# A delta-rule attention and an FFN on one core: raw weights decoded through PSUM, norm temporaries in PSUM, a new written order

## The chip, the core and the metric

The kernel runs on one core of one Trainium2 chip. Five engines work side by side, each through its own instruction queue in order: TensorE (PE, matmuls, with its weight loads shown apart as PEld), VectorE (DVE), ScalarE (ACT), GpSimd (POOL) and SyncE (SP, which here only issues DMAs). Matmuls write to PSUM, which has eight banks of 512 float32 values in each of 128 partitions; all other data lies in SBUF. The metric is device time in microseconds, lower is better. The kernel before takes 664.81 us (median of 3 runs, 664.76 to 665.1).

## The reference

An attention with a state that is updated token by token, and behind it a feed-forward layer on the attention's output:

```python
def _attn_ref(q, k, v, beta):                      # 4 x 8 heads, 768 tokens, 48 features
    k_n = k / (np.linalg.norm(k, axis=-1, keepdims=True) + 1e-06)
    state = np.zeros((B, H, D, D)); y = np.zeros_like(q)
    for t in range(S):
        kt, vt, bt = (k_n[:, :, t], v[:, :, t], beta[:, :, t, None])
        y[:, :, t] = np.einsum('bhd,bhde->bhe', q[:, :, t], state)
        v_old = np.einsum('bhde,bhd->bhe', state, kt)
        state = state + bt[:, :, :, None] * np.einsum('bhd,bhe->bhde', kt, vt - v_old)
    return y

def _moe_ref(x, w_in, w_out):                      # 3072 tokens, 384 -> 2048 -> 384
    h = x @ w_in
    sp = np.maximum(h, 0.0) + np.log1p(np.exp(-np.abs(h)))     # softplus
    g = h * erf(sp)
    return (g @ w_out).astype(np.float32)
```

All of it is float32, and the order of the tokens matters: the state of a head at token t depends on all earlier tokens.

## The kernel before, in words

**Attention.** The 768 tokens are cut into 12 chunks of 64 (index c). For a chunk the kernel forms the Gram matrices of the keys (`gram_mm`, "pg") and of queries with keys ("pq"), scales them by beta and the inverse norms (`gram_a`, `gram_d`), solves a triangular system for each head (POOL's `solve_row`, 31 rows for each pair of chunks; for the first two chunks instead DVE's `first_row`, 15 steps), puts the blocks of the inverse together (`merge_e`, `merge_z`, `merge_m`) and then walks the chain of states: for each chunk and batch (index j, 48 in all) `chain_u`, `chain_s` and `chain_y` on PE, each followed by a step on DVE or ACT (`chain_u2`, `chain_s2`, `chain_y2`).

**Norms.** `norm_sq` (ACT) squares the keys of a chunk, `norm_sum` (DVE) sums the squares, and `norms` (DVE, 18 small operations on 128x32 values for two chunks) takes a bit-trick start value and three root iterations, and from them `nm` (the norm), `ga` and `gn` (beta over the squared norm, plus and minus). The group of two chunks is called sg, 0 to 5.

**Weights.** w_in and w_out come in as float32 pairs read as int64, in 12 blocks each of 128x512 pairs (512 KB). A block goes through four steps: `w_load` (DMA into a raw buffer), `w_mask` (ACT, a Prelu that turns the high words into float values, line 539), `w_low` (DVE, shift of the low words, line 543), `w_bits` (DVE, joins both, line 547). After three blocks `w_sum` (ACT) takes the absolute maximum. Then come a scale (`w_max`, `w_all`, `w_scale`), and 16 parts of each weight are split into two float16 halves: `w_hi`, and for w_in `w_dif` (two float32 matmuls and one float16 on PE into PSUM) and `w_lo` (a copy out).

**FFN.** 12 groups of 256 tokens (index g). `x_tr` transposes the attention's output, `x_all`/`x_scale` scale it, `x_hi` and `x_lo` split it into float16 halves; `ffn1` makes 16 slices of h (nine matmuls each, line 678), two slices in one PSUM tile called ph; ACT takes softplus (`e_sp`, line 704) and erf (`e_erf`, line 709), DVE or ACT copies h (`h_out`, lines 691 and 689), DVE multiplies (`e_mul`) and splits (`e_split`, `e_rest`); `ffn2` multiplies by w_out into the banks pr (lines 739 to 741) and `ffn_out` and `ffn_store` finish.

**PSUM.** Pool psa has three banks (tag pa), ps1 has two (tag ph), and three banks pr0 to pr2 are held throughout. Tag ph serves `warm` (one tile that all the filler matmuls of the start write, held until the last of them), the tiles wd of `w_dif`, and the tiles ph of `ffn1`. An engine that touches a bank waits for another engine that still uses that bank.

**Tables of ACT.** Softplus lies in one table set and erf in another. `table(i)` adds a load where its own record says that another set is loaded; it is called in `e_sp`, `e_erf` and `w_sum`, not in `w_mask`.

**Order.** Every step is recorded as an event, and the table ORDER, a permutation of all 2531 events, sets the order in which they are issued; each engine, SP's DMA queue included, takes its own in that order. Filler matmuls (`fill`, 150 of them, line 143) stand among PE's events of the first 80 us.

Of the kernel before, what the change touches and what calls it, by code (L numbers as in the profile page):

```python
# [7 lines left out]
F32 = mybir.dt.float32  # L8
F16 = mybir.dt.float16
BF16 = mybir.dt.bfloat16  # L10
I32 = mybir.dt.int32
# [4 lines left out]
P = 128  # L16
# [23 lines left out]
WO = 0.6  # L40
WD = 0.4
RI = "HLHLHLHLHLLL"
RO = "HLHLHLHLHLLL"
LMI = [5, 3] * 8
LMO = [0] * 16
WG = 3
LID = 0.12
LOD = 0.25
HQ = (0, 4)
SPA = (2, 6)  # L50
EB = 4
HB, LB = 5, 7
# [20 lines left out]
def delta_ffn_kernel(ctx, tc, kT, qT, ktok, vtok, btok, w_in, w_out, cst, out):  # L73
# [99 lines left out]
    def load_q(c):  # L173
        for hb in range(2):
            sp.dma_start(qp[c % 2][hb][rd(hb)], qT[c, hb])

    def norm_sq(c):
        s = st[c]
        if c < 2:
            s["sq"] = early(4160 + 1024 * c, 1024)[:, :BP * D].rearrange("p (a d) -> p a d", a=BP)  # L180
        else:
            s["sq"] = at.tile([P, BP, C], F32, tag="A", name=f"sq{c}")[:, :, :D]
        se.activation(s["sq"], s["k"], AF.Square, bias=0.0, scale=1.0)

    nt = {}

    def norm_sum(c):
        sg, i = divmod(c, 2)
        if sg not in nt:
            nt[sg] = sm.tile([P, 2, BP], F32, tag="n2", name=f"n2_{sg}")  # L190
        ve.tensor_reduce(nt[sg][:, i, :], st[c]["sq"], axis=AX.X, op=ALU.add)

    def norms(sg, w):

        w = slice(0, 2)
        names = ("ri", "t1", "nm", "ga", "gn")
        if sg not in nb:
            nb[sg] = [sm.tile([P, 2, BP], F32, tag=k, name=f"{k}{sg}") for k in names]
        n2, be = nt[sg][:, w], be_t[sg][:, w]
        ri, t1, nm, ga, gn = (x[:, w] for x in nb[sg])  # L200
        ii = ri.bitcast(I32)
        ops = [lambda: ve.tensor_scalar(n2, n2, 1e-30, None, op0=ALU.max),

               lambda: ve.tensor_scalar(ii, n2.bitcast(I32), 1, None, op0=ALU.logical_shift_right),
               lambda: ve.tensor_scalar(ii, ii, -1.0, float(0x5F3759DF), op0=ALU.mult, op1=ALU.add)]
        for _ in range(3):
            ops += [lambda: ve.tensor_tensor(t1, ri, ri, op=ALU.mult),
                    lambda: ve.scalar_tensor_tensor(t1, t1, -0.5, n2, op0=ALU.mult, op1=ALU.mult),
                    lambda: ve.scalar_tensor_tensor(ri, t1, 1.5, ri, op0=ALU.add, op1=ALU.mult)]
        ops += [lambda: ve.tensor_tensor(nm, n2, ri, op=ALU.mult),  # L210
                lambda: ve.tensor_scalar(nm, nm, 1e-6, None, op0=ALU.add),
                lambda: ve.reciprocal(ri, nm),
                lambda: ve.tensor_tensor(t1, be, ri, op=ALU.mult),
                lambda: ve.scalar_tensor_tensor(gn, t1, -1.0, ri, op0=ALU.mult, op1=ALU.mult),
                lambda: ve.tensor_scalar(ga, gn, -1.0, None, op0=ALU.mult)]
        for i in range(2):
            st[2 * sg + i].update((k, x[:, i, :]) for k, x in zip(names, nb[sg]))
        return ops
# [292 lines left out]
    def stage(nm, i, n=RW):  # L511

        return wb[nm].rearrange("p a b -> p (a b)")[:, DM + i * n:DM + i * n + n]
# [21 lines left out]
    def w_mask(nm, i):  # L535


        hf = wt[nm]["raw", i][:, :, 1].bitcast(F32)
        se.activation(stage(nm, i), hf, AF.Prelu, bias=0.0, scale=2.0 ** -112, alpha=2.0 ** 32)
# [5 lines left out]
    def w_bits(nm, i):  # L545
        ai = stage(nm, i).bitcast(I32)
        ve.scalar_tensor_tensor(ai, ai, 3, wt[nm]["raw", i][:, :, 0], op0=ALU.logical_shift_left, op1=ALU.bitwise_or)
# [450 lines left out]
```

## Time and profile before

| | before |
|---|---|
| median of 3 runs | 664.81 us (664.76 to 665.1) |
| the profiled execution | 663.63 us, its span 661.9 us |
| granted TensorE clock, mean | 0.986 |
| PE busy | 630.6 us (95%), 9866 matmuls |
| DVE busy | 468.8 us (71%), 1032 instructions |
| ACT busy | 468.6 us (71%), 694 instructions |
| POOL busy | 357.7 us (54%), 524 instructions |
| moved by DMA | 56.20 MB |

Line numbers (L678) are those of the kernel before. A row of the group view reads: line, engine, operation, output<-input, shapes, count, then the group's busy time, the mean duration of one in ns, and the idle time of the engine just before them with what ended it. A row of a window reads: the stretch, its length, then the busy time and count of PE, PEld, DVE, ACT and POOL, the granted clock, the share of the DMA engines and GB/s. A row of the timeline or of the chain that ended last begins with the start and the duration, both in us.

### The profile page before, as it was taken

The page shows a single profiled execution, that of the slowest core. Times are in us where ns is not written, and L with a number is a line of the kernel's source. Part 1 is how long each engine was busy: PE and PEld are TensorE (multiplying, and loading weights), DVE is VectorE, ACT ScalarE, POOL GpSimd, SP SyncE. Part 2 cuts the span into 40 slices and gives each one's busy share as a digit, 9 for nine tenths or more (in the row PEclk, how much of TensorE's full clock was granted, in tenths as well). Part 3 has the DMA queues.
Part 4 walks back from the last instruction along what each step waited for, and adds up shares of the span by engine and source line. Part 5 has one row for each costly group of instructions (what it writes and reads, how often), then busy time and mean ns, then how long its engine had stood idle before and what let it go on. Part 6 is the DMA issues. An engine that isn't in the chain of part 4 may idle for free.

```text
span 661.9 us, 22889 instructions
## 1 busy us (share of the span) xinstructions
PE 630.6 (95%) x9866; PEld 481.5 (73%) x9866; DVE 468.8 (71%) x1032; ACT 468.6 (71%) x694; POOL 357.7 (54%) x524
## 2 busy tenths in 40 slices
PE   6788999999999999999899999999999999999996
PEld 4556668777768787777687677887776787777763
DVE  4977869878877886668766778875649765657541
ACT  2187898999768897656684677667566788768860
POOL 5081289779997259782489942239972321211322
PEclk8878999999999999999999999999999999999999
DMA  9875761673121740504622241531204210000102
GB/s 246 283 214 164 195 182 34 127 140 77 39 90 29 164 106 3 126 16 112 146 46 56 76 87 26 127 78 31 52 18 104 46 39 13 14 1 1 37 1 48
DMA packets 76421, 56.20 MB, mean 85 GB/s; under 512 B 57184, under 2 KB 66528, under 8 KB 76320
## 3 DMA queue, kind: packets, MB, share of 16 engines
q1 hardware_dynamic: 76320, 54.74, 33.9%
q8 instruction: 77, 1.26, 0.8%
q14 instruction: 24, 0.20, 0.1%
HBM read 42.14 MB, written 12.58 MB: 83 GB/s over the span
## 4 chain that ended last, share of the span: by engine, by line
PE 53%; DVE 16%; ACT 13%; POOL 7%; issue 5%; DMA 4%; SPq 1%; POOLq 0%; DVEq 0%; ACTq 0%
PE ph L678 17%; PE pr L739 7%; PE pr L741 6%; PE pr L740 6%; DVE H L713 3%; POOL xb L364 3%; ACT L128 3%; POOL tmp L363 2%; PE warm L143 2%; ACT L L709 2%; PE pc L488 2%; DVE H L691 2%; PE pm L426 1%; DVE z L467 1%; ACT L L704 1%
## 5 line engine op out<-in xcount | busy, mean ns | idle before, releaser
L678 PE MATMUL ph<-xh,w_in 128*128 128x256 f16 x1152 | 207.6, 273 | 2.7 <-ACT L L704 2.3
L678 PEld LDWEIGHTS <-w_in 128*128 128x128 f16 x1728 | 164.9, 98 | 30.2 <-issue 3.8
L128 ACT ACT_TABLE_LOAD x131 | 168.1, 1283 | 2.2
L728 POOL TENSOR_TENSOR L<-H,L 128x512 f16<-128x512 f32 x72 | 85.3, 1195 | 147.6 <-DVE L L724 96.7
L678 PE MATMUL ph<-xl,w_in 128*128 128x256 f16 x576 | 157.0, 273 | 0.0
L741 PE MATMUL pr<-w_out,L 128*128 128x384 f16 x384 | 125.2, 326 | 0.7 <-POOL L L728 0.7
L739 PE MATMUL pr<-w_out,L 128*128 128x384 f16 x384 | 125.4, 327 | 0.0
L740 PE MATMUL pr<-w_out,L 128*128 128x384 f16 x384 | 125.2, 326 | 0.0
L448 POOL TENSOR_TENSOR z<-v,nm 64x192 f32<-64x192 f32 x96 | 56.4, 587 | 104.6 <-DMA v<-vtok 59.8
L704 ACT ACTIVATE L<-ph,xct 128x512 f32<-128x512 f32 x96 | 65.7, 687 | 53.5 <-DVE H L691 48.5
L364 POOL TENSOR_TENSOR xb<-xb,tmp 128x31 f32<-128x31 f32 (+15 forms) x155 | 95.0, 613 | 12.2
L363 POOL TENSOR_TENSOR tmp<-gb,xb 128x31 f32<-128x31 f32 (+15 forms) x155 | 85.1, 549 | 27.0 <-DMA gb<-d 16.7
L713 DVE TENSOR_TENSOR H<-H,L 128x512 f32<-128x512 f32 x96 | 75.6, 795 | 27.9 <-ACT L L709 23.6
L691 DVE TENSOR_SCALAR H<-ph 128x512 f32<-128x512 f32 x72 | 49.2, 685 | 36.0 <-PE ph L678 27.5
L709 ACT ACTIVATE L<-L 128x512 f32<-128x512 f32 x96 | 58.6, 627 | 0.8
L741 PEld LDWEIGHTS <-L 128*128 128x128 f16 x384 | 37.6, 98 | 26.1 <-POOL L L728 1.4
L739 PEld LDWEIGHTS <-L 128*128 128x128 f16 x384 | 37.5, 98 | 21.8
L740 PEld LDWEIGHTS <-L 128*128 128x128 f16 x384 | 37.6, 98 | 20.8
L467 DVE TENSOR_TENSOR z<-pc,ga 64x192 f32<-64x192 f32 x80 | 28.4, 355 | 27.5 <-PE pc L461 26.0
L661 ACT ACTIVATE xh<-pt,xsx 64x128 f16<-64x128 f32 (+1 forms) x72 | 26.0, 395 | 24.6 <-PE pt L645 12.7
L143 PE MATMUL warm<-zero 128*128 128x384 f16 x158 | 35.0, 373 | 3.3 <-issue 2.2
L724 DVE CAST L<-H 128x512 f16<-128x512 f32 x72 | 35.7, 500 | 1.4
(157 smaller groups left out, 968.5 us busy)
## 6 DMA issues: line engine op xcount, KB each, us to landing
raw_in<-w_in SPq DMA_DIRECT2D x12, 512.0 KB, 8.0
raw_out<-w_out SPq DMA_DIRECT2D x12, 512.0 KB, 5.0
d<-A SPq DMA_DIRECT2D x20, 256.0 KB, 3.2
kpg<-kT SPq DMA_DIRECT2D x24, 192.0 KB, 4.5
k<-ktok SPq DMA_DIRECT2D x12, 384.0 KB, 4.6
v<-vtok SPq DMA_DIRECT2D x48, 96.0 KB, 2.7
qp<-qT SPq DMA_DIRECT2D x24, 192.0 KB, 3.5
out<-ob SPq DMA_DIRECT2D x48, 96.0 KB, 2.2
```

Of the source, the lines that this page charges most:

```text
L128: se.add_instruction(mybir.InstLoadActFuncSet(name=nc.get_next_instruction_name(), act_func_set_id=i, ins=[], outs=[]))
L363: ge.tensor_tensor(tv, G[:, s, s + 1:].unsqueeze(1).broadcast_to([P, ncol, nr]), Xv[:, :, s:s + 1].broadcast_to([P, ncol, nr]), op=ALU.mult)
L364: ge.tensor_tensor(Xv[:, :, s + 1:], Xv[:, :, s + 1:], tv, op=ALU.add)
L678: te.matmul(ph, w[:, i, kt * P:kt * P + P], G[x][:, :, ksl], start=(m == 0), stop=(m == 8))
L691: ve.tensor_scalar(dst, src, HSC, None, op0=ALU.mult)
L704: se.activation(unit("L", g, u), G["ph", u], AF.Softplus, bias=0.0, scale=G["ct"])
L709: se.activation(Lu, Lu, AF.Erf, bias=0.0, scale=1.0)
L713: ve.tensor_tensor(Hu, Hu, unit("L", g, u), op=ALU.mult)
L728: (ge if (g * NFF // EU + u) % GLM else ve).tensor_tensor(G["gl", u], unit("H", g, u), G["gh", u], op=ALU.subtract)
L739: te.matmul(G["po"][a], gh[:, o, asl], wout_h[:, i, :], start=(i == 0), stop=False)
L740: te.matmul(G["po"][a], gh[:, o, asl], wout_l[:, i, :], start=False, stop=False)
L741: te.matmul(G["po"][a], gl[:, o, asl], wout_h[:, i, :], start=False, stop=(i == NFF - 1))
```

## The change

Three things change. `w_mask` writes its result no longer into the weight's own SBUF space but into a PSUM tile of tag ph (both weights, PM), and `w_bits` takes it from there. The squared norms (n2) and the temporary t1 lie in unused columns of a bank pr (`ntmp`); since no operation then has two PSUM inputs, the root iteration multiplies in another order, with the same count of operations, and `ga` is formed directly. And the table ORDER is another one. All 2531 events are the same.

```diff
-ORDER = (1,56,2,4,88,42,3,23,13,36,5,7,27,6,44,9,10,273,52,130,14,57,37,24,25,43,17, ...
+ORDER = (1,63,7,42,5,14,6,3,8,27,4,77,9,19,65,37,48,64,49,43,2,57,58,44,529,66,10, ...
...
+PM = ('in', 'out')
...
+    def ntmp(sg, k):
+        return pr[sg % PB][:, 384 + 32 * k:416 + 32 * k].rearrange("p (i a) -> p i a", i=2)
+
     def norm_sum(c):
...
-            nt[sg] = sm.tile([P, 2, BP], F32, tag="n2", name=f"n2_{sg}")
+            nt[sg] = ntmp(sg, 0)
...
-            nb[sg] = [sm.tile([P, 2, BP], F32, tag=k, name=f"{k}{sg}") for k in names]
+            nb[sg] = [sm.tile([P, 2, BP], F32, tag=k, name=f"{k}{sg}") if k != "t1" else ntmp(sg, 1) for k in names]
...
-            ops += [lambda: ve.tensor_tensor(t1, ri, ri, op=ALU.mult),
-                    lambda: ve.scalar_tensor_tensor(t1, t1, -0.5, n2, op0=ALU.mult, op1=ALU.mult),
+            ops += [lambda: ve.tensor_tensor(t1, n2, ri, op=ALU.mult),
+                    lambda: ve.scalar_tensor_tensor(t1, t1, -0.5, ri, op0=ALU.mult, op1=ALU.mult),
                     lambda: ve.scalar_tensor_tensor(ri, t1, 1.5, ri, op0=ALU.add, op1=ALU.mult)]
-        ops += [lambda: ve.tensor_tensor(nm, n2, ri, op=ALU.mult),
-                lambda: ve.tensor_scalar(nm, nm, 1e-6, None, op0=ALU.add),
+        ops += [lambda: ve.tensor_tensor(t1, n2, ri, op=ALU.mult),
+                lambda: ve.tensor_scalar(nm, t1, 1e-6, None, op0=ALU.add),
...
-                lambda: ve.scalar_tensor_tensor(gn, t1, -1.0, ri, op0=ALU.mult, op1=ALU.mult),
-                lambda: ve.tensor_scalar(ga, gn, -1.0, None, op0=ALU.mult)]
+                lambda: ve.tensor_tensor(ga, t1, ri, op=ALU.mult),
+                lambda: ve.scalar_tensor_tensor(gn, t1, -1.0, ri, op0=ALU.mult, op1=ALU.mult)]
...
-        se.activation(stage(nm, i), hf, AF.Prelu, bias=0.0, scale=2.0 ** -112, alpha=2.0 ** 32)
+        if nm in PM:
+            dst = wt[nm]["p", i] = ps1.tile([P, RW], F32, tag="ph", name=f"wm_{nm}{i}")
+        else:
+            dst = wt[nm]["p", i] = stage(nm, i)
+        se.activation(dst, hf, AF.Prelu, bias=0.0, scale=2.0 ** -112, alpha=2.0 ** 32)
...
-        ve.scalar_tensor_tensor(ai, ai, 3, wt[nm]["raw", i][:, :, 0], op0=ALU.logical_shift_left, op1=ALU.bitwise_or)
+        ve.scalar_tensor_tensor(ai, wt[nm]["p", i].bitcast(I32), 3, wt[nm]["raw", i][:, :, 0], op0=ALU.logical_shift_left, op1=ALU.bitwise_or)
```

The lines of the changed kernel are up to eight further down: `w_mask` is 547, `w_bits` 555, `ffn1` 686, softplus 712, erf 717.

**ACT in the decoding of w_in.** The first rows are the kernel before, the next the changed one, at the place where ACT decodes the middle blocks of w_in (raw_in) between the small copies that build the first inverse (xm).

```order
L539 ACTIVATE w_in_100<-raw_in11_272 128x512
L539 ACTIVATE w_in_100<-raw_in7_385 128x512
L344 COPY w_out_101<-pw1_508 128x256
L539 ACTIVATE w_in_100<-raw_in8_328 128x512
L333 COPY xm0_0_90<-w_out_101 32x16x32
```

```order
L547 ACTIVATE wm_in8_650<-raw_in8_173 128x512
L547 ACTIVATE wm_in11_657<-raw_in11_328 128x512
L547 ACTIVATE wm_in9_674<-raw_in9_275 128x512
L547 ACTIVATE wm_in6_683<-raw_in6_372 128x512
L337 COPY xm0_1_91<-w_out_101 32x16x32
```

Each output is now a tile wm of tag ph. While `warm` holds one of the two banks, all tiles wm lie in the other one (in the built program 16 in a row, the 12 of w_in and the first 4 of w_out), so a `w_mask` follows the `w_bits` of the block before it.

**DVE at the same place, changed kernel.** The rows that free the bank, each with w_low (line 551) of other blocks between:

```order
L555 SCALAR_TENSOR_TENSOR w_in_100<-wm_in0_440,raw_in0_268 128x512
L551 TENSOR_SCALAR raw_in2_422<-raw_in2_422 128x512
L551 TENSOR_SCALAR raw_out10_259<-raw_out10_259 128x512
L555 SCALAR_TENSOR_TENSOR w_in_100<-wm_in2_572,raw_in2_422 128x512
L551 TENSOR_SCALAR raw_in4_270<-raw_in4_270 128x512
L555 SCALAR_TENSOR_TENSOR w_in_100<-wm_in8_650,raw_in8_173 128x512
L551 TENSOR_SCALAR raw_in11_328<-raw_in11_328 128x512
L555 SCALAR_TENSOR_TENSOR w_in_100<-wm_in11_657,raw_in11_328 128x512
```

What moved: mask and join of one block now alternate across the two engines, block by block, where ACT could run ahead.

**ACT at the first softplus.** Before, from the last sum ahead of the first softplus (L0 from ph0) to the first table load behind it:

```order
L554 ACTIVATE raw_out2_675,mx_out_111<-w_out_101 128x1536
L611 CAST w_in_100<-wd_in11_1680 128x384
L128 ACT_TABLE_LOAD
L704 ACTIVATE L0_0_1741<-ph0_1_1687,xct0_1576 128x512
L704 ACTIVATE L0_0_1741<-ph0_0_1729,xct0_1576 128x512
L689 ACTIVATE H0_0_1724<-ph0_0_1729 128x512
L183 ACTIVATE sq5_1785<-k5_1389 128x16x48
L704 ACTIVATE L0_1_1813<-ph0_2_1758,xct0_1576 128x512
L611 CAST w_in_100<-wd_in12_1787 128x384
```

And in the changed kernel, from the same load on:

```order
L129 ACT_TABLE_LOAD
L712 ACTIVATE L0_0_1772<-ph0_1_1729,xct0_1612 128x512
L547 ACT_TABLE_LOAD
L547 ACTIVATE wm_out9_1787<-raw_out9_1563 128x512
L277 COPY qp0_0_86<-pq2_0_1691 64x512
L277 COPY qp0_1_87<-pq2_0_1691 64x512
L497 COPY y5_1822<-pr2_83 128x192
L712 ACT_TABLE_LOAD
L712 ACTIVATE L0_0_1772<-ph0_0_1760,xct0_1612 128x512
L697 ACTIVATE H0_0_1770<-ph0_0_1760 128x512
L547 ACT_TABLE_LOAD
L547 ACTIVATE wm_out7_1841<-raw_out7_1559 128x512
```

The masks of blocks 9 and 7 of w_out now stand between softpluses; behind the last row come one squaring, a fourth load at line 712 and the softplus of ph0_2. The four loads at lines 547 and 712 are not `table`'s (that is line 129): they are put in when the program is built, since Prelu is not in softplus's set. The built program has 136 table loads; it had 132.

2 lines of the change are left out of this document (1 added, 1 removed).

## The prediction

> **What bounds the kernel now.** I read the busy times first, then windows by stage, then the groups of ACT and DVE with what they waited for, and last the chain at the start.
>
> ```profile
> PE 630.6 (95%) x9866; PEld 481.5 (73%) x9866; DVE 468.8 (71%) x1032; ACT 468.6 (71%) x694; POOL 357.7 (54%) x524
> 0.00:33.00 33.00, 23.65 (x461) 16.10 (x465) 22.20 (x67) 6.21 (x9) 9.61 (x18) 0.90 0.91 265
> 33.00:94.20 61.20, 55.91 (x1342) 37.86 (x1330) 45.88 (x107) 49.61 (x91) 29.82 (x46) 0.92 0.72 198
> 97.00:129.00 32.00, 31.88 (x470) 26.02 (x469) 28.75 (x74) 29.73 (x50) 26.34 (x43) 1.00 0.32 68
> 100.00:650.00 550.00, 538.94 (x7970) 420.05 (x7968) 394.97 (x846) 406.48 (x582) 312.10 (x453) 1.00 0.28 62
> ```
>
> From 100 to 650 us PE is idle for 550 - 538.94 = 11.1 us only, and its work there is the same in both kernels. So the time is set by when PE gets to the FFN, and by what makes it wait afterwards. From 33 to 94 us PE looks busy too, but part of that is filler:
>
> ```profile
> L143 PE MATMUL warm<-zero 128*128 128x384 f16 x158 | 35.0, 373 | 3.3 <-issue 2.2 <-DVE zero L134 1.1
> 99.22 0.27 PE L678 MATMUL ph<-xh,w_in 128*128 128x256 f16 x1
> 94.24 1.10 ACT L661 ACTIVATE xh<-pt,xsx 128x256 f16<-128x256 f32 x3 [0.36 <-DVE xsx L528]
> 128.70 0.33 PE L739 MATMUL pr<-w_out,L 128*128 128x384 f16 x1
> ```
>
> The first real FFN matmul starts at 99.22 us, five microseconds after `x_hi` starts on ACT at 94.24. In front of it ACT worked 49.61 of 61.2 us, so it idled 11.6. What it waited for:
>
> ```profile
> ACT T L405 <- PE pe L400: 4.4, 1, 4.4
> ACT w_out L344 <- PE pw L340: 2.8, 1, 2.8
> ACT w_in L611 <- PE wd_in L604: 1.2, 1, 1.2
> ACT w_in L590 <- ACT xm L417: 0.8, 1, 0.8
> ```
>
> Two waits of 4.4 and 2.8 us are for PE, whose chain there is fillers and instruction issue:
>
> ```profile
> 34.06 1.73 PE warm L143 x10
> 36.14 2.44 issue
> 49.41 2.15 issue
> 51.56 3.66 PE warm L143 x13
> ```
>
> From 97 to 129 us, where the FFN begins, PE is full (31.88 of 32) and ACT has 2.3 us to spare (29.73 of 32). This is the stretch in which a late ACT makes a late PE.
>
> **The change part by part.** All sums are made against the profiled execution, 663.63 us (span 661.9 and 1.7 around it); the median of the runs is 664.81, so 1.2 is added at the end.
>
> *Norms in PSUM.* The 18 operations stay 18. Early, alone, one takes 0.19 us; later it is longer:
>
> ```profile
> L207 DVE TENSOR_TENSOR t<-ri 128x32 f32<-128x32 f32 x18 | 5.6, 310 | 0.5
> L207 DVE TENSOR_TENSOR t<-ri 128x32 f32<-128x32 f32 x3 | 0.6, 191 | 0.1
> L631 DVE TENSOR_REDUCE xm<-sp 128x1 f32<-128x128 f32 x12 | 3.4, 284 | 4.3 <-PE sp L523 4.3
> L499 DVE TENSOR_REDUCE mg<-y 128x1 f32<-128x192 f32 x48 | 14.7, 343 | 0.9 <-ACT y L493 0.7
> ```
>
> If all 18 of line 207 ran at 0.19, DVE would save 18 x 0.12 = 2.1 us over the run, and something on its neighbours. A PSUM input has a price too: no row shows such a small operation on PSUM, and the nearest is the reduction at line 631, 284 ns for 128 values of PSUM against 343 for 192 of SBUF, so between nothing and some 0.06 us each. For sg 0, which lies on the chain, that is 0 to 18 x 0.06 = 1.1 us lost. For sg 1 to 5 it is DVE time, and DVE idles 155 us between 100 and 650. I take nothing, cover: DVE's idle time; if that cover is gone, a few us at most.
>
> *`w_bits` from PSUM.* On DVE:
>
> ```profile
> L547 DVE SCALAR_TENSOR_TENSOR w_in<-w_in,raw_in 128x512 int32<-128x512 int32 x12 | 10.3, 868 | 2.3 <-ACT w_in L539 1.9
> L547 DVE SCALAR_TENSOR_TENSOR w_out<-w_out,raw_out 128x512 int32<-128x512 int32 x12 | 9.1, 770 | 0.5
> L547 DVE SCALAR_TENSOR_TENSOR w_in<-w_in,raw_in x12: 680/692/1569, 24.7 to 62.1; 128x512 int32<-128x512 int32 x12
> ```
>
> Median 692 ns, mean 868 and 770: a few are stretched. At the median throughout DVE saves 12 x 0.18 + 12 x 0.08 = 3.1 us. DVE has 15.3 us of idle time from 33 to 94 us (61.2 - 45.88), so I take none of it as time.
>
> The Trainium skill ("SBUF — State Buffer", Who interferes with whom) says that a VectorE instruction with two SBUF inputs contends with GpSimd's reads, and one with a single SBUF input does not. The stretched `w_bits` and root operations fit that; by it the whole 3.1 us would be saved, which changes no term here since DVE is not what x waits for.
>
> *Start, up to 33 us.* SP now issues both key chunks, beta and both kf ahead of any 512 KB weight block. Before, ACT's first mask held the squares back:
>
> ```profile
> 0.74 0.87 SPq L232 DMA_DIRECT2D kpg<-kT  x2
> 4.11 0.42 PE L247 MATMUL pg<-kpg 48*32 48x64 f32 x2
> 2.12 5.77 DMA raw_in<-w_in
> 7.92 0.66 ACT w_in L539
> 8.58 0.74 ACT w_out L183
> 15.67 2.66 DVE w_out L264 x8
> 18.35 2.12 DVE w_out L316
> 30.82 1.86 DVE w_out L327
> ```
>
> The first kf came 3.4 us after its issue at 0.74; keys issued as the fourth load, at about 2.6, can then be there at 6.0 at the earliest, where the squares started at 8.58: at most 2.6 us earlier, at least nothing, and I take 1.9. DVE's order then differs in front of the two transposes that PE waits for (lines 327 and 329; the one at 30.82 took 1.86 us): two of eight `gram_d` moved behind, two `w_bits` (0.7 each, a row above) moved behind the transposes, and the transpose that `first_w` needs is now the second instead of the first, some 1.9 us that take back the gain. So `first_w` starts at about 32.7 us as before (30.82 + 1.86), while two `w_bits` are still owed. I count zero, bounds -1.5 and +1.
>
> *ACT from 33 us to `x_hi`.* By the two orders ACT has nearly the same work left there:
>
> ```profile
> L611 ACT CAST w_in<-wd_in 128x384 f16<-128x384 f32 x16 | 7.5, 476 | 1.3 <-PE wd_in L604 1.2
> L333 ACT COPY xm<-w_out 32x512 f32<-32x512 f32 x8 | 4.9, 612 | 0.1
> ```
>
> It is one more `norm_sq` (0.74 as in the row at 8.58), one more `w_lo` (line 611, 0.48) and one `first_copy` less (line 333, 0.61), about 50.2 instead of 49.6 us. What changes is idle time. It gains a wait: with one bank for the masks, a mask that stands next to a mask on ACT waits for the `w_bits` between them, about 0.7 us. In the order that is blocks 8 to 11, 11 to 9 and 9 to 6 of w_in, and 3 to 5, 5 to 2 and 8 to 0 of w_out: six, 4.2 us. Behind such a mask stand the copies that build xm, and PE waits for those. It loses a wait: only 68 fillers instead of 96 stand in front of `merge_e(0)` on PE, 28 x 0.17 to 0.33 = 5 to 9 us of PE, more than the 4.4 us that ACT waited for exactly that. The second mask can start when the first `w_bits` is done behind the transposes, at 32.7 + 0.7 = 33.4. I keep 2.0 us of small waits for `w_dif` and its like as now (1.2 + 0.8) and 1.5 for PE's issue stalls. So `x_hi` starts at 33.4 + 50.2 + 4.2 + 2.0 + 1.5 = 91.3 instead of 94.24: **-2.9 us**. Bounds: with the six handoffs alone 87.8 (-6.4); with all of the present 11.6 us of idle time and the handoffs on top 99.4 (+5.2).
>
> *The start of the FFN.* The groups:
>
> ```profile
> L128 ACT ACT_TABLE_LOAD x131 | 168.1, 1283 | 2.2
> L704 ACT ACTIVATE L<-ph,xct 128x512 f32<-128x512 f32 x96 | 65.7, 687 | 53.5 <-DVE H L691 48.5 <-PE ph L678 4.2
> L539 ACT ACTIVATE w_out<-raw_out 128x512 f32<-128x512 f32 x12 | 7.6, 672 | 0.0
> 108.42 1.28 ACT L128 ACT_TABLE_LOAD   x1
> 109.72 0.63 ACT L709 ACTIVATE L<-L 128x512 f32<-128x512 f32 x1
> ```
>
> Four table loads more, 4 x 1.283 = 5.1 us, and one mask more than before behind `x_hi` (block 7, line 539), less the one `w_lo` that is already done (0.48): 5.3 us more on ACT in a stretch where it had 2.3 to spare and PE nothing. Queued behind the masks on ACT are the softplus of ph0_0 and ph0_2 and the `w_lo` of parts 12 and 13; PE's `w_dif` and `ffn1` wait for those. The two masks also hold a bank ph each, from the mask to the end of its `w_bits`, 0.67 + 0.69 = 1.4 us, in which `ffn1` has one bank. Bounds: 5.3 - 2.3 = 3.0 if ACT's spare time takes its share; 5.3 + 2 x 1.4 = 8.1 if the bank waits come on top. I take the loads, **+5.1**, near the middle, since loads and held banks overlap in part.
>
> The Trainium skill ("ScalarE: Activation LUTs", What ACT_TABLE_LOAD costs) gives 1283 ns for a load and some 1380 ns of drain with it, 2.66 us a switch. The trace has the 1283, but the erf at 109.72 starts 0.02 us after its load ended. By the page the four would cost 10.6 us and the sum come out 5.5 higher; the measurement decides.
>
> *The rest of the order.* Outside that stretch the table loads are as many as before. PE's 11.1 us of idle time from 100 to 650 are many small waits:
>
> ```profile
> PE ph L678 <- ACT L L704: 2.3, 4, 0.8
> PE pt L644 <- DVE A L258: 1.5, 2, 1.1
> ```
>
> In another order these are other waits. `norm_sum` of sg 4 and 5 also waits for the last `ffn2` of the group whose bank it uses, and the `h_out` behind it on DVE with it. I take **-0.5** (`gram_a` of chunk 3 comes earlier, so POOL's solve does), bounds -4 and +4.
>
> Sum: -2.9 + 5.1 - 0.5 = +1.7: the profiled execution 665.3, the median 664.81 + 1.7 = **666.5 us**.
>
> **The rivals.**
>
> *Faster: ACT's gain at the start outweighs the loads.* If only the six handoffs remain (-6.4) and ACT's spare time takes its share of the loads (+3.0): -3.4, **661.4 us**. For it speaks that 7.2 of ACT's 11.6 idle us are waits for PE, which now has fewer fillers in its way; against it that 97 to 129 us is already full on PE.
>
> *No change: PE takes the delay back.* If the waits of 100 to 650 us shrink because PE arrives later than the engines that feed it, 2 of the 11.1 us are enough: +1.7 - 2 = about 0, **664.8 us**. Against it: these waits are at most 1.1 us each, and most are for steps that themselves follow PE.
>
> *Clearly slower: the one bank decides the start.* If PE's issue stalls (2.44 and 2.15 us) fall again in front of `merge_e(0)` and `first_x`, ACT keeps some 4.5 of its waits for PE on top of the handoffs: `x_hi` comes at 94.9 to 95.8, about +1.5, and with the loads +6.6: **671 us**. It decides from the point where a mask waits longer than the 0.7 us of one `w_bits`.
>
> **How the numbers follow.** About 0.2% (1.3 us) is what a measurement here can tell from no change. Forecast 0.31, faster 0.31, no change 0.25, clearly slower 0.13. The forecast alone spans 665 to 669; the range over the cases is 661 to 671, since rivals on both sides hold most of the chance. Both slower cases make 0.44; no change 0.25; faster 0.31.
>
> **What would show it.** In the changed profile: 136 table loads; the first `ffn1` near 96 instead of 99.2 us; in the group of `w_mask` idle time that DVE's `w_bits` ended, about 4 us; PE idle for 4 us or more in the 35 us behind the first `ffn1`, with waits for softplus, line 712, or for line 555; the first `ffn2` at 127 to 130 us, with less PE work done in front of it. The forecast is wrong if the first `ffn1` comes before 93 or after 99 us, if PE stays full behind it in spite of the loads, or if PE's idle time from there to 650 us differs from 11 us by more than four beside that stretch.

## The result, and the profile after

The changed kernel takes 672.13 us (median of 11 runs, 666.76 to 674.36); the kernel before, beside it on the same chips, 664.05 us (11 runs). The ratio is 1.0115, 95% interval 1.0092 to 1.0139: slower by 1.15%, some 7.6 us. Forecast were 666.5 us and a range up to 671; the sign was right, the size too small by nearly six microseconds. The profiled execution takes 671.29 us with a span of 669.5, against 663.63 and 661.9 before.

PE by stage, first before and then after, each cut at the first `ffn1`, 34 us behind it and near the end. The columns are the stretch, its length, PE's busy time and count, the granted clock, the share of the DMA engines and GB/s:

```profile
0.00:99.22 99.22, 84.59 (x1854) 0.91 0.76 214
99.22:134.00 34.78, 34.66 (x497) 1.00 0.42 86
134.00:650.00 516.00, 505.06 (x7482) 1.00 0.27 61
650.00:661.90 11.90, 6.30 (x39) 0.91 0.24 54
```

```profile
0.00:103.46 103.46, 87.40 (x1871) 0.90 0.73 206
103.46:138.00 34.54, 29.65 (x421) 1.00 0.33 78
138.00:657.00 519.00, 509.12 (x7534) 1.00 0.27 61
657.00:669.50 12.50, 7.40 (x46) 0.96 0.14 31
```

From the first `ffn1` to the end PE does the same work: 34.66 + 505.06 + 6.30 = 546.0 us before, 29.65 + 509.12 + 7.40 = 546.2 after. So the 7.6 us split into three: the first `ffn1` starts 4.2 us later (103.46 instead of 99.22); in the 34.5 us behind it PE idles 4.9 us instead of 0.1; and from there to the end it idles 15.0 us instead of 16.5.

The starts of `x_hi` and of the first `ffn1` (timeline of the changed kernel), and what ACT waited for from 33 us to `x_hi` (waits: in total, times, longest):

```profile
99.56 2.22 ACT L669 ACTIVATE xh<-pt,xsx 128x256 f16<-128x256 f32 x6 [0.17 <-DVE xsx L532]
103.46 0.27 PE L686 MATMUL ph<-xh,w_in 128*128 128x256 f16 x1
```

```profile
ACT wm_in L547 <- DVE w_in L555: 4.6, 6, 1.6
ACT T L409 <- PE pe L404: 2.9, 1, 2.9
ACT wm_out L547 <- DVE w_out L555: 2.5, 3, 1.0
ACT xm L421 <- PE pz L417: 1.4, 1, 1.4
```

`x_hi` comes at 99.56 us instead of 94.24, where 91.3 was forecast. The handoffs of the masks on their one bank are there, nine instead of six, 7.1 us instead of 4.2. Behind the first `ffn1` PE waits for what was named:

```profile
PE ph L686 <- DVE w_out L555: 2.7, 2, 1.3
PE wd_in L611 <- ACT L L712: 0.9, 1, 0.9
PE spout L527 <- DVE m_out L566: 0.8, 1, 0.8
PE wd_in L611 <- ACT w_in L619: 0.6, 1, 0.6
```

On DVE the joins and the root iteration are faster than before (groups: count, busy time, mean ns, idle time in front):

```profile
L555 DVE SCALAR_TENSOR_TENSOR w_in<-wm_in,raw_in 128x512 int32<-128x512 int32 x12 | 8.3, 688 | 3.8 <-ACT wm_in L547 3.4
L211 DVE TENSOR_TENSOR pr<-pr,ri 128x32 f32<-128x32 f32 x18 | 3.5, 196 | 2.0 <-PE pr L478 1.5
L213 DVE SCALAR_TENSOR_TENSOR ri<-pr,ri 128x32 f32<-128x32 f32 x18 | 3.4, 191 | 0.6
```

A `w_bits` takes 688 ns on average where it took 868, the iteration's operations 0.19 to 0.20 us, where the same groups of before had means of 231 to 349 ns. That gain did not reach the end here; the last experiments show where it can.

### The profile page after: what moved, and what is told of

Its sections match the earlier page's. It is cut to its first block, busy times and chain, and to the rows that moved or that the text cites. A ratio compares the mean times of both kernels' runs of the same rounds, so it can differ in the third digit from the quotient of the medians.

```text
span 669.5 us, 22923 instructions
## 1 busy us (share of the span) xinstructions
PE 633.6 (95%) x9866; PEld 485.2 (72%) x9866; DVE 467.1 (70%) x1032; ACT 474.9 (71%) x698; POOL 356.8 (53%) x524
## 3 DMA queue, kind: packets, MB, share of 16 engines
q8 instruction: 77, 1.26, 0.8%
## 5 line engine op out<-in xcount | busy, mean ns | idle before, releaser
L736 POOL TENSOR_TENSOR L<-H,L 128x512 f16<-128x512 f32 x72 | 87.0, 1220 | 129.2 <-DVE L L732 118.7
L452 POOL TENSOR_TENSOR z<-v,nm 64x192 f32<-64x192 f32 x96 | 54.1, 564 | 113.5 <-DMA v<-vtok 59.3
L367 POOL TENSOR_TENSOR tmp<-gb,xb 128x31 f32<-128x31 f32 (+15 forms) x155 | 88.0, 568 | 42.0 <-DMA gb<-d 32.6
L368 POOL TENSOR_TENSOR xb<-xb,tmp 128x31 f32<-128x31 f32 (+15 forms) x155 | 92.9, 599 | 12.1
L732 DVE CAST L<-H 128x512 f16<-128x512 f32 x72 | 41.1, 572 | 1.8
L471 DVE TENSOR_TENSOR z<-pc,ga 64x192 f32<-64x192 f32 x80 | 28.4, 355 | 18.2 <-PE pc L465 16.5
```

Of the source, the lines that this page charges most:

```text
L367: ge.tensor_tensor(tv, G[:, s, s + 1:].unsqueeze(1).broadcast_to([P, ncol, nr]), Xv[:, :, s:s + 1].broadcast_to([P, ncol, nr]), op=ALU.mult)
L368: ge.tensor_tensor(Xv[:, :, s + 1:], Xv[:, :, s + 1:], tv, op=ALU.add)
L452: ge.tensor_tensor(zz[j % 6][h1, :, hb, :], vt[j][h1], st[c]["nm"][h1, cs].unsqueeze(2).broadcast_to([C, NP, D]), op=ALU.mult)
L736: (ge if (g * NFF // EU + u) % GLM else ve).tensor_tensor(G["gl", u], unit("H", g, u), G["gh", u], op=ALU.subtract)
```

## The experiments

All ratios are to the kernel before on the same chip. "SBUF" and "PSUM" say where masks and norms lie.

| run | edit | median, before beside it | ratio (95%) |
|---|---|---|---|
| changed | | 672.13, 664.05 | 1.0115 (1.0092 to 1.0139) |
| e1 | new order, old code | 670.49, 662.38 | 1.0126 (1.0083 to 1.0169) |
| e2 | changed, masks in SBUF | 671.24, 662.38 | 1.0138 (1.0094 to 1.0183) |
| e3 | changed, norms in SBUF | 669.75, 662.38 | 1.0106 (1.0065 to 1.0148) |
| e4 | changed, two masks ahead of `ffn1` | 668.80, 662.38 | 1.0099 (1.0060 to 1.0137) |
| e5 | old code, old order up to `x_hi` | 668.06, 661.84 | 1.0091 (1.0058 to 1.0125) |
| e6 | old code, new order up to `x_hi` | 665.57, 661.84 | 1.0040 (1.0015 to 1.0065) |
| e7 | changed, 18 fillers out | 666.48, 661.84 | 1.0055 (1.0032 to 1.0077) |
| e8 | old order, norms in PSUM | 662.34, 661.84 | 1.0002 (0.9980 to 1.0025) |
| e9 | changed, load_q(11) early | 669.11, 662.87 | 1.0105 (1.0072 to 1.0138) |
| e10 | changed, two masks under erf's table | 665.79, 662.87 | 1.0050 (1.0021 to 1.0078) |
| e11 | before, 18 fillers out | 663.92, 662.87 | 1.0026 (1.0007 to 1.0045) |
| e12 | e7, e9 and e10 together ("mended") | 662.22, 662.87 | 0.9996 (0.9978 to 1.0014) |
| e13 | mended, w_out's masks in SBUF | 661.88, 661.96 | 1.0004 (0.9980 to 1.0029) |
| e14 | mended order, old code | 666.92, 661.96 | 1.0077 (1.0053 to 1.0100) |
| e15 | e5 with the mask of block 9 late, load_q early | 667.42, 661.96 | 1.0073 (1.0047 to 1.0099) |
| e16 | e13 with norms in SBUF | 666.91, 663.09 | 1.0059 (1.0033 to 1.0085) |
| e17 | e13, w_max(out) ahead of three norm operations | 663.11, 663.09 | 1.0002 (0.9980 to 1.0024) |
| e18 | e17 with the 18 fillers | 665.67, 663.09 | 1.0045 (1.0016 to 1.0075) |

### Which of the three changes costs: e1, e2, e3, e8

e1 takes the kernel before and exchanges only the table:

```diff
-ORDER = (1,56,2,4,88,42,3,23,13,36,5,7,27,6,44,9,10,273,52,130,14,57,37,24,25,43,17, ...
+ORDER = (1,63,7,42,5,14,6,3,8,27,4,77,9,19,65,37,48,64,49,43,2,57,58,44,529,66,10, ...
```

> The kernel before with the new order alone: masks and norms in SBUF as before. The changed kernel started its first ffn1 at 103.46 us (before 99.22) and lost 4.9 us of PE in the 34.5 us behind it. Theory M (the masks' one bank makes ACT wait, 7.1 us for w_bits): without the PSUM masks x_hi comes at 92 to 95, first ffn1 at 97 to 100; the table loads stay, so PE idles 2 to 4 us at the FFN's start; 664 to 667 us. Rival N (norms in PSUM: DVE waits 2.7 and 1.5 us for PE matmuls in the same bank): the same for this kernel, since the norms are in SBUF too. Rival O (the order itself, PE's queue of w_dif and fillers): first ffn1 stays at 102 to 104, 669 to 672 us.

e2 keeps the changed kernel and puts the masks back:

```diff
-PM = ('in', 'out')
+PM = ()
```

> The changed kernel with both kinds of masks written to SBUF again; norms stay in PSUM, the new order stays. Theory M: no wait of ACT for w_bits, x_hi at 92 to 95, first ffn1 97 to 100, the 2.7 us of ffn1's waits for w_bits gone, 664 to 667 us. Rival N: DVE still waits 4 us for PE in the bank of the norms, first ffn1 at 102 to 104; only the bank waits at the FFN's start go (2 to 3 us): 668 to 670 us. Rival O: first ffn1 at 102 to 104, 668 to 671 us.

e3 puts only norms and temporary back, with the new arithmetic:

```diff
-            nt[sg] = ntmp(sg, 0)
+            nt[sg] = sm.tile([P, 2, BP], F32, tag="n2", name=f"n2_{sg}")
-            nb[sg] = [... if k != "t1" else ntmp(sg, 1) for k in names]
+            nb[sg] = [sm.tile([P, 2, BP], F32, tag=k, name=f"{k}{sg}") for k in names]
```

> The changed kernel with the squared norms and the temporary in SBUF tiles again; masks stay in PSUM, order and arithmetic stay. Theory M: x_hi and first ffn1 as in the changed kernel, 671 to 673 us. Rival N: the 2.7 and 1.5 us of DVE's waits for PE go, first ffn1 at 99 to 101, 667 to 669 us. Rival O: 671 to 673 us.

e8 is the changed code with PM = () under before's table. In that order `norm_sum(2)` writes 16 columns of a bank that still holds the product "pq" of chunk 0, four events ahead of `gram_p(0,1)`, which reads it, so part of that product is lost. e8 leaves out the wait that would keep it; its time is that of these instructions and waits only.

> The kernel before in its own order, with only the squared norms and the root iteration's temporary in PSUM (and the new form of the iteration); masks in SBUF. The prediction priced this at 0: within 0.2%, 661 to 664 us beside 662.4. Rival N (the bank waits of DVE cost what they last): 664 to 667 us.

The order alone costs 1.26%, as much as the whole change. Masks in SBUF do not give it back (1.0138), norms in SBUF do not either (1.0106), and norms in PSUM under the old order cost nothing that shows (1.0002); the intervals of e1 to e3 are 0.4% wide to each side. Masks in PSUM under the old order were not tried: there a mask would wait for a bank that is only freed behind it. So theory M (the masks' one bank) and theory N (the waits in the norms' bank) fall. What became of the 7.1 us of handoffs, e2 shows in ACT's waits over the same stretch:

```profile
ACT T L409 <- PE pe L404: 4.7, 2, 3.0
ACT xm L359 <- DVE xm L359: 3.1, 2, 2.7
ACT w_out L348 <- PE pw L344: 2.5, 1, 2.5
ACT w_in L619 <- PE wd_in L612: 2.1, 4, 0.6
```

No wait for `w_bits` is left, and ACT idles as long for other things, most of all for PE: 15.2 of the 65.7 us from 33 us to `x_hi`, against 15.5 of 66.6 in the changed kernel. The handoffs filled time in which ACT waits in any case.

### Where the order costs: e5, e6

Both have the old code and a spliced table:

```diff
+ORDER = (events of before's table up to the first x_hi, then the rest in the new order)   # e5
+ORDER = (events of the new table up to the first x_hi, then the rest in before's order)   # e6
```

> The kernel before (masks and norms in SBUF) with a spliced order: before's order up to the first x_hi, and behind it all that is left in the new order. The new order alone cost 1.26% (some 8 us). Theory L (the loss is made ahead of x_hi: PE reaches w_dif(0) behind seven more fillers, merge_z(1) and chain_y(2)): first ffn1 at 98 to 100 as before, 663 to 665 us. Theory F (the loss is made behind x_hi, where the four table loads make PE's w_dif wait 3.6 us and PE's granted clock halves after the gap): first ffn1 at 98 to 100, but the loss stays, 668 to 671 us. If both parts share it: 665 to 668 us.

> The mirror of it: the kernel before with the new order up to the first x_hi, and behind it all that is left in before's order (132 table loads). Theory L: first ffn1 at 100 to 104, 668 to 671 us. Theory F: first ffn1 at 100 to 102, no gap of 3 us behind it, 663 to 666 us. If both share it: 665 to 668 us.

Both parts cost: 0.40% (2.7 us) ahead of `x_hi`, 0.91% (6.0 us) behind it, together 1.31% against the 1.26% of e1. The part behind `x_hi` does not hold all four table loads here: before's lead has the mask of block 7 in it already, so in e5 only the mask of block 9 stands between softpluses, and the profile shows two loads more than before, not four. Six microseconds are more than two loads of 1.28. The single profiles are a poor guide to the first part: with the same order up to `x_hi` it started at 94.24 us in the profile of before, at 98.0 in e5 and at 91.3 in e8, with a mean granted clock of 0.92, 0.85 and 0.95 between 33 us and there.

### Ahead of x_hi: e7, e11

`w_dif(0)` needs the scale of w_in: DVE's `w_max`, then `w_all` on PE (spin). Before (`w_max`, spin, `w_dif(0)`), and in the changed kernel `w_max` (timelines):

```profile
70.62 0.16 DVE L558 TENSOR_REDUCE m_in<-mx_in 128x1 f32<-128x4 f32 x1 [0.66 <-ACT raw_in L554]
70.88 0.46 PE L523 MATMUL spin<-ident,m_in 128*128 128x128 f32 x2 [0.21 <-PE warm L143]
74.21 0.91 PE L603 MATMUL wd_in<-w_in,dg 128*128 128x384 f32 x2
```

```profile
71.82 0.15 DVE L566 TENSOR_REDUCE m_in<-mx_in 128x1 f32<-128x4 f32 x1
```

Before, DVE waits for ACT and PE is at `w_all` 0.3 us after `w_max` starts; in the changed kernel PE gets there 2.1 us after it. What stands on PE from there to `w_dif(0)` in the changed kernel:

```profile
73.91 0.38 PE L527 MATMUL spin<-ident,m_in 128*128 128x128 f32 x2
74.13 0.49 PE L144 MATMUL warm<-zero 128*128 128x384 f16 x2
74.55 2.08 PE L255 MATMUL pg<-kpg 48*64 48x64 f32 x64
76.56 1.31 PE L144 MATMUL warm<-zero 128*128 128x384 f16 x7
77.80 1.20 PE L417 MATMUL pz<-xm,T 32*32 32x32 f32 x64
78.93 0.67 PE L492 MATMUL pr<-z,qp 128*64 128x48 f32 x16
79.43 0.64 PE L465 MATMUL pr<-z,xm 128*64 128x48 f32 x16
80.54 0.91 PE L611 MATMUL wd_in<-w_in,dg 128*128 128x384 f32 x2 [0.47 <-DVE w_out L555]
81.29 0.33 PE L612 MATMUL wd_in<-w_in,ng 128*128 128x384 f16 x1
81.45 1.95 PE L144 MATMUL warm<-zero 128*128 128x384 f16 x11
```

PE runs from 73.91 to 83.4 us with one gap of 0.47 us; it is a full queue, and `w_dif(0)` is in it behind seven fillers more than before (139 against 132), and behind `merge_z(1)`, which before stood ahead of `w_all`. The gap of 0.47 us is for a `w_bits`: `warm` holds one bank up to its last filler, so `w_dif(0)` takes the masks' bank.

The same shows in every profile (starts in us, then the time from the start of `w_max` to that of `w_all` and of the first `ffn1`):

| lead, up to `x_hi` | profiles | `w_max` starts | to `w_all` | to the first `ffn1` |
|---|---|---|---|---|
| old | before, e8, e11, e15 | 67.8 to 70.7 | 0.2 to 0.3 | 28.0 to 29.2 |
| old, half clock in part of it | e5 | 70.2 | 0.3 | 33.4 |
| new, all fillers | changed, e1, e2, e3, e6, e9, e10, e18 | 68.8 to 71.8 | 1.4 to 2.1 | 30.3 to 32.4 |
| new, 18 fillers out | e7, e12 to e14, e16, e17 | 68.2 to 73.8 | 1.6 to 2.1 | 29.5 to 30.4 |
| new, two masks more in it | e4 | 71.0 | 2.2 | 34.6 |

So with the new order `w_max` comes no earlier, and PE is later behind it. From `w_dif(0)` to `x_hi` pass 18.6 to 20.0 us in all profiles but that of e5 (21.6). e7 takes 18 fillers out, the seven and the eleven of the last row:

```diff
-ORDER = (..., fill x7, merge_z(1), chain_y(2), chain_u(3), w_dif(in,0), fill x11, w_dif(in,1), ...)
+ORDER = (..., merge_z(1), chain_y(2), chain_u(3), w_dif(in,0), w_dif(in,1), ...)
```

> The changed kernel without the 18 fillers (matmuls on zeros whose result nothing reads) that stand on PE from w_all of w_in to w_dif(1): seven ahead of w_dif(0), eleven ahead of w_dif(1). If PE's own queue sets x_hi (w_dif(0) plus 19 us in every run so far): x_hi 2.5 to 3.2 us earlier than the changed kernel's 99.56, first ffn1 near 100.5, 667 to 669 us. If ACT's work sets it, as the prediction reckoned: x_hi within 0.5 us of 99.56, 671 to 673 us. A third way: the fillers hold the granted clock, and without them PE runs at half speed for one window more in front of x_hi: x_hi no earlier, 671 to 674 us.

From 1.15% to 0.55%, about 4 us for 18 fillers of some 0.17 us. In its profile `w_dif(0)` comes at 77.1 us instead of 80.5 and `x_hi` at 97.0 instead of 99.6; the gain lies ahead of `w_dif(0)`, and is more there than seven fillers, in part because the changed kernel's profile has a stretch of half clock from 65 to 71 us that this one lacks. Behind `w_dif(0)` eleven fillers fewer won nothing: 19.9 us instead of 19.0, and PE waits 2.6 us there for `w_lo`, which is ACT's. So PE's queue is on the path up to `w_dif(0)`, and behind it no longer. The edit does a second thing: `warm` gives its bank back some 10 us earlier, and the wait for a `w_bits` is gone. e17 and e18 below differ in the same fillers with w_out's masks in SBUF, where no mask holds a bank at that time, and the fillers cost 0.4% there too. e11 takes the same 18 events out of the kernel before:

> The kernel before with the same 18 fillers taken out as in the cut of the changed kernel (there 0.6% faster). If PE's queue is what sets x_hi in this kernel too: x_hi 1.5 to 3 us earlier than 94.2, 659 to 660.5 us beside 661.8. If ACT or the solve sets it: 661 to 663 us. If the fillers hold the clock: more halved windows ahead of x_hi, 662 to 665 us.

It is slower by 0.26% (0.07 to 0.45). In before's order all 18 stand behind `w_dif(0)` (12, 5 and 1 of them), so nothing was taken from in front of it: `w_dif(0)` comes at 74.3 us as before (74.2). `x_hi` came at 93.4 us, 0.8 earlier. Why the whole is slower stays open; no profiled row shows it.

### Behind x_hi: e4, e10, e9

e4 moves the two masks that cause the four table loads ahead of the first `ffn1`:

```diff
-..., ffn1(0,2), ffn1(0,3), ..., e_sp(0,1), w_mask(out,9), ..., e_sp(0,0), w_mask(out,7), ..., e_sp(0,2), ...
+..., w_mask(out,9), w_sum(out,0), w_mask(out,7), ffn1(0,2), ffn1(0,3), ..., e_sp(0,1), e_sp(0,0), e_sp(0,2), ...
```

> The changed kernel with only the masks of w_out blocks 9 and 7 (with their w_low and w_bits) moved ahead of the first ffn1, so that they no longer stand between softpluses: 132 table loads instead of 136. If the four loads (5.1 us of ACT) and the bank held by the two masks make PE's 4.9 us of idle time at the FFN's start: idle there 0 to 1.5 us, x_hi some 1 us later at most, 667 to 669 us. If PE's waits there come from something else (w_dif, the order), 671 to 673 us as the changed kernel.

It won nothing that the intervals show (1.0099 against 1.0115). The loads are gone, but the masks now stand ahead of the last `w_lo`, and PE waits for that: 1.4 us at the last `w_dif` ahead of the first `ffn1` and 1.3 us in front of that `ffn1`, which starts 6.8 us behind `x_hi` instead of 3.9. Behind these waits the clock was halved for some 7 us. e10 puts them behind the third softplus instead, under the table that erf loads anyway:

```diff
-..., e_sp(0,1), w_mask(out,9), ..., e_sp(0,0), w_mask(out,7), ..., e_sp(0,2), w_sum(out,2), e_erf(0,1), ...
+..., e_sp(0,1), e_sp(0,0), e_sp(0,2), e_erf(0,1), w_mask(out,7), w_mask(out,9), w_sum(out,2), ...
```

> The changed kernel with 132 table loads: e_erf of part 1 stands right behind the third softplus, and the masks of w_out blocks 9 and 7 (with w_bits) right behind it, under the table that it loads. In the run with the masks moved ahead of the first ffn1 the four loads were gone too, but 1.3 us of masks then stood ahead of the last w_lo, and it won 0.2% only. If the four loads (5.1 us of ACT) are what PE waits for behind x_hi: PE idle in the 34.5 us behind the first ffn1 under 1.5 us instead of 4.9, first ffn1 as in the changed kernel, 667 to 669 us. If PE's waits there come from the order of the other work: 670 to 672 us.

From 1.15% to 0.50%, 4.3 us, of the size of the 5.1 us of the loads. In its profile PE idles 2.3 us in the 34.5 us behind the first `ffn1`, where it idled 4.9. Of its waits there one is left:

```profile
PE ph L686 <- DVE w_out L555: 2.3, 1, 2.3
```

It is the bank that the two masks hold. In e2, where the masks lie in SBUF and the loads are there, the waits are one too, as long as the changed kernel's waits for `w_bits` and softplus together (2.7 + 0.9; start, duration, and in brackets the wait):

```profile
116.98 1.21 PE L611 MATMUL wd_in<-w_in,dg 128*128 128x384 f32 x2 [3.57 <-ACT L L712]
118.44 1.95 PE L492 MATMUL pr<-z,qp 128*64 128x48 f32 x32
```

So by these two profiles the held bank was no cost beside the loads in the changed kernel: it only gave part of the same wait another name. e9 moves one load:

```diff
-..., chain_y2(39), ..., from_blocks(11), put_blocks(11), ..., from_blocks2(11), load_q(11), ...
+..., chain_y2(39), load_q(11), ..., from_blocks(11), put_blocks(11), ..., from_blocks2(11), ...
```

> The changed kernel with one load moved: load_q of the last chunk (11), whose gram PE waited 1.4 and 0.34 us for at 532 us, stands on SP's queue some 45 places earlier (behind chain_y2(39)), about as far ahead of its use as before. In every run with the new order behind x_hi but one, PE's granted clock was halved for 3.4 to 6.8 us right behind that wait. If wait and halving belong together: no wait for qp there, no halved window at 535 to 540, 2 to 4 us less than the changed kernel's 671 to 672: 668 to 670 us. If the window comes from elsewhere, only the wait goes, or moves to the next one: 670 to 672 us.

The wait for qp and the halved window behind it are gone from that place, but in its profile another gap, of 2.2 us, had such a window, at 242 us, and the time is the same within the interval (1.0105).

### Mended, and what PSUM is worth then: e12 to e18

e12 has the edits of e7, e9 and e10 together:

> The changed kernel with the three edits together: 18 fillers out, load_q(11) early, e_erf and the two masks behind the third softplus. If they add up (4 + 3 + 3 us): 660 to 663 us, as the kernel before, since what is left of the change (PSUM) is worth nothing. If PE's waits only move to the next late engine: 664 to 667 us.

Alone they won 0.60, 0.10 and 0.65%, together they win 1.19%: 0.9996, the time of the kernel before. From there e13 frees the bank, e14 takes the mended order back to the old code, and e15 mends the part behind `x_hi` of e5:

```diff
-PM = ('in', 'out')
+PM = ('in',)          # e13; e14 and e15: before's code, no PM, norms in SBUF
```

> The mended kernel (fillers out, load_q early, two masks late) with the masks of w_out in SBUF again; masks of w_in and the norms stay in PSUM. Behind the first ffn1 it still had one wait of PE of 2.3 us for a bank that the two late masks hold up to the end of their w_bits, and a halved window of 3.4 us right behind it. If that wait is the price of the masks in PSUM: it is gone, PE idle under 0.8 us in the 34.5 us behind the first ffn1, 658 to 661 us. If the bank only stands in for the softplus that precedes it: a wait of 1.5 to 3 us for ACT in its place, 661 to 664 us.

> The mended order under the code before the change: all masks and the norms in SBUF. If PSUM is worth nothing but for that one held bank: as the run with w_out's masks in SBUF, 658 to 661 us. If masks or norms in PSUM are worth something on DVE (the stretched w_bits are gone with them): 1 to 3 us more than that run. If they cost: 1 to 3 us less.

> The code before the change, before's order up to the first x_hi with all its fillers, and behind it the new order with load_q early and the two masks behind the third softplus. The unmended splice was 0.91% slower than the kernel before. If the four loads and the wait for qp are all that the new order costs behind x_hi: 0 to 0.2% slower, 661 to 663 us beside 662.5. If the new order behind x_hi costs beside them: 0.4 to 0.8% slower, 665 to 667 us.

e13 is level with the kernel before, e14 and e15 are 0.7% slower. So the loads and the load of qp do not explain what the order costs under the old code, and the PSUM placement is worth something after all. e15 has no extra load left, and wins on e5 no more than the intervals allow (1.0073 against 1.0091). What PE waits for behind the first `ffn1` there is `w_max` of w_out:

```profile
PE spout L523 <- DVE m_out L558: 4.0, 1, 4.0
```

In e5 this wait was 2.0 us, in e14 it is 5.0; the kernel before has none. So the new order makes two engines late at the start of the FFN, ACT by the loads and DVE by `w_max`, and taking one away uncovers the other. e16 is e13 with the edit of e3:

> The mended kernel with w_out's masks in SBUF (661.9 us, level with the kernel before), and the squared norms and the temporary in SBUF too; w_in's masks stay in PSUM. The mended order with all of it in SBUF was 0.73% slower than that, with a wait of PE of 5.0 us for w_all of w_out (2.2 with the norms in PSUM): on DVE the 18 root operations of chunks 4 and 5 in front of it took 7.5 us instead of 5. If the norms' place makes that difference: 665 to 667 us, PE's wait for w_all 4 to 5 us. If the place of w_in's masks makes it: 661 to 663 us.

It is the norms: 1.0059 with them in SBUF, 1.0004 in PSUM, with intervals apart. PE's waits behind the first `ffn1`, first e16, then e13:

```profile
PE spout L527 <- DVE m_out L566: 4.4, 1, 4.4
```

```profile
PE spout L527 <- DVE m_out L566: 2.2, 1, 2.2
```

The two waits differ by 2.2 us of the 0.55%, which is 3.6; the clock behind the first `ffn1` was lower too (0.90 in the 34.5 us, 0.95 in e13). PE stands at `w_all` of w_out and waits for `w_max`, which stands on DVE behind the 18 root operations of chunks 4 and 5. Some of them in e16, then some in e13 (timelines of DVE):

```profile
118.88 0.58 DVE L212 SCALAR_TENSOR_TENSOR t<-t,ri 128x32 f32<-128x32 f32 x1
119.50 0.65 DVE L213 SCALAR_TENSOR_TENSOR ri<-t,ri 128x32 f32<-128x32 f32 x1
120.18 0.19 DVE L211 TENSOR_TENSOR t<-n,ri 128x32 f32<-128x32 f32 x1
120.41 0.51 DVE L212 SCALAR_TENSOR_TENSOR t<-t,ri 128x32 f32<-128x32 f32 x1
```

```profile
112.04 0.68 DVE L209 TENSOR_SCALAR ri<-ri 128x32 int32<-128x32 int32 x1
112.99 0.20 DVE L212 SCALAR_TENSOR_TENSOR pr<-pr,ri 128x32 f32<-128x32 f32 x1
113.22 0.19 DVE L213 SCALAR_TENSOR_TENSOR ri<-pr,ri 128x32 f32<-128x32 f32 x1
115.68 0.62 DVE L217 TENSOR_TENSOR pr<-be,ri 128x32 f32<-128x32 f32 x1
```

The sequence takes 7.0 us in e16 (117.5 to 124.5) and 5.0 in e13 (111.6 to 116.6), and POOL is at its solve all the while (6.2 us and 4.6 us busy). In e13 only operations without a PSUM input are still stretched, lines 209 and 217; those with one take 0.18 to 0.20, and in e16 the same lines take 0.19 at one time and up to 0.67 at another. The Trainium skill ("SBUF — State Buffer", Who interferes with whom) says that a VectorE instruction with two SBUF inputs contends with a GpSimd one that reads SBUF, and one with a single SBUF input, outside the two-port modes, does not; lines 212, 213 and 217 agree with it. Line 209 has one SBUF input; it is a tensor_scalar, which the same section counts among the forms that can be in a two-port mode.

e17 puts `w_max(out)` ahead of `norm_ops(2,5)` and `gram_a(4,0)`, e18 puts the fillers back:

```diff
-..., norm_ops(2,4), norm_ops(2,5), gram_a(4,0), h_out(6), w_max(out), ...
+..., norm_ops(2,4), h_out(6), w_max(out), norm_ops(2,5), gram_a(4,0), ...
```

> The mended kernel with w_out's masks in SBUF and norms in PSUM, with w_max of w_out put ahead of the last three root operations and of gram_a of chunk 4 on DVE. If PE's wait of 2.2 us for w_all, and the halved window behind it, come from DVE's queue alone: wait under 0.5 us, no halved window there, 658 to 660.5 us, faster than the kernel before by 0.2 to 0.6%. If ACT's w_sum sets it: 661 to 662.5 us.

> The same with the 18 fillers put back. Cutting them won 0.6% in the changed kernel and lost 0.26% in the kernel before. If PE's queue ahead of x_hi is what counts: 1.5 to 3 us slower than without them, 660 to 663 us. If the fillers pay for themselves through the clock: the same or faster.

e17 is no faster than e13 (1.0002): the wait went from 2.2 to 1.5 us. e18 is 0.4% slower than e17 (the intervals just touch), so under the new order the fillers cost again, here with no mask of w_out in PSUM. No version beats the kernel before; e12, e13 and e17 are level with it.

## Why the prediction was right or wrong

**Norms in PSUM, 0.** Right for the kernel before's order (e8, within 0.25%) and for the changed kernel (e3, within 0.4%). The price of a PSUM operand was in its bounds, 0.01 us an operation (0.20 against 0.19). The cover named was DVE's idle time; it holds where nothing urgent stands behind the norms. In the mended order `w_max` does, the cover is gone, and the placement earns 0.55%. Not seen was that DVE now waits for PE in the bank of chunks 2 and 3, 2.7 and 1.5 us, for matmuls into other columns; it cost nothing that e3 could show. The Trainium skill ("PSUM — Partial Sum Buffer", PSUM bank collisions raise a hardware error) says to guard PSUM by bank and quadrant, not by address; these waits are such guards.

**w_bits from PSUM, 0.** Right: the mean fell from 868 and 770 to 688 and 686 ns, and e2 gives nothing back.

**Start to 33 us, 0.** Right: `first_w` begins at 32.83 us, before at 32.81.

**ACT from 33 us to x_hi, -2.9.** This is the step that failed. The forecast reckoned `x_hi` from ACT's work and idle time, took 28 fillers as gone from in front of `merge_e(0)`, and counted 4.2 us of handoffs. ACT's work was nearly right (51.1 us, 50.2 reckoned); its idle time was not, 15.5 us where 7.7 were reckoned: 7.1 for `w_bits` instead of 4.2, and 8.4 for other engines, most of it for PE, instead of 3.5. `merge_e(0)` did come earlier, at 44.97 instead of 55.15 us, but the fillers were not gone: they stand behind it, and in both orders all 150 stand ahead of `x_all`. What had no term is PE's queue from `w_max` to `w_dif(0)`: in e6, which measures the new lead alone, `w_max` starts at 70.3 us as before (70.6), and from there to the first `ffn1` pass 31.4 us instead of 28.6. Its runs cost 2.7 us instead of earning 2.9. The fillers are part of that (e7, e18), the moved `merge_z(1)` another. How much of it the halved clock carries is open: the median of the mean clocks of e6's runs is that of the kernel before's beside them (0.986).

**Start of the FFN, +5.1.** Right in size (4.9 us of idle time in place of 0.1), and for this kernel in cause: e10 removes the four loads and wins 4.3 us. The table-load price of the trace, 1.28 us, carries it; twice that was not seen. The bank waits, which the bounds added on top, were no extra that shows. Not seen was the second late engine: with the norms in SBUF this part of the order costs nearly as much without the extra loads (e15 beside e5), since PE then waits for `w_max` of w_out.

**Rest of the order, -0.5.** The waits became fewer by 1.5 us in the profile; no run measures this term alone.

With +2.7 in the place of -2.9 the sum is 2.7 + 5.1 - 0.5 = 7.3, and 664.81 + 7.3 = 672.1 us; that this meets the measured 672.13 so closely is luck, since e6's interval alone is 1.0 to 4.3 us and comes from the old code. The rival that came nearest in time, one bank decides the start (671), had its condition met, masks waited up to 1.6 us. Its first half holds, ACT kept waits for PE on top of the handoffs; that the bank decides is refuted by e2. Of the marks named, the first `ffn1` (near 96, and the forecast wrong if after 99) said at once which step it was.

## What to carry to other kernels

Before a stage's end is reckoned from one engine's work, count what stands ahead of that end in every queue: work that is only moved behind a nearer milestone is still ahead of the farther one, and fillers count as work. An instruction that is off the path can be made faster for nothing until an order puts something urgent behind it; so the worth of a placement and of an order are measured together, not each in the other's old surroundings. Where two functions of ACT need different tables, an instruction of the one between two of the other costs two loads; the place that won here was behind a load that is due anyway, not simply earlier.

## What the runs showed of the hardware

The granted clock halves for stretches of some 3.4 us, or about twice that, behind a gap of PE. In the changed kernel PE waited 1.42 and 0.34 us for qp (the two rows), and these are the windows ahead of, in and behind the stretch that followed:

```profile
533.38 0.30 PE L255 MATMUL pq<-qp,kpq 48*64 48x64 f32 x2 [1.42 <-DMA qp<-qT]
534.01 2.53 PE L255 MATMUL pq<-qp,kpq 48*64 48x64 f32 x62 [0.34 <-DMA qp<-qT]
```

```profile
525.00:532.00 7.00, 6.96 (x105) 1.00 0.58 113
535.60:539.00 3.40, 3.40 (x29) 0.53 0.00 0
539.00:543.00 4.00, 4.00 (x114) 1.00 0.23 52
```

By these rows such a stretch of 3.4 us costs about 1.7 us of PE where PE is the bound. The Trainium skill ("TensorE: Matmul & The Clock Gate", Part 1: The HAM clock gate) says that the clock falls to half after an idle window of some 3.4 us; here gaps of 1.3 to 2.2 us sufficed in several runs (1.42 above, 1.34 and 2.20 in e9, 2.22 in e13). Other gaps of that size left the clock at 1.00: two of 1.3 us behind the first `ffn1` of the changed kernel, one of 2.1 us at 243 us, and one of 1.49 in e9. A gap of that size can halve the clock or not. The mean clock differs from run to run, and roughly with it the time: the changed kernel's runs had mean clocks from 0.967 (674.36 us) to 0.986 (666.84 us), with a median of 0.979, where the kernel before's had medians of 0.986 to 0.987 beside the experiments. The difference of 0.007 over 670 us is 4.7 us, an estimate of what the clock alone could carry if PE had been the bound all the time; where in a run the stretches fell is known for the profiled executions only, and there part of them lies over fillers.
